# Weight loads and fp32 rows in pieces, each held until a step of the work (attention and squared-ReLU FFN on a normalised input)

## The chip, the core and the metric

The kernel runs on one core of a Trainium2 chip. Its engines are TensorE (PE, with its weight loads as PEld), VectorE (DVE), ScalarE (ACT), GpSimd (POOL) and SyncE (SP), which only issues transfers. The metric is the device time of one execution in microseconds (us). The median of three runs of the kernel before is 748.19 us (748.0 to 749.2).

## The reference

One layer norm feeds an attention with 32 query heads that share one key and one value head, and a feed-forward network with a squared ReLU; both are added to the input x. S = 2048 rows, D = 640, head size 20, F = 1536, all bfloat16.

```python
xn = layernorm(x)
q = (xn @ wq) in 32 heads of 20;  k = xn @ wk;  v = xn @ wv
p = softmax(q k^T / sqrt(20));    o = p v  -> [S, 640] @ wo
h = xn @ w1 + b1;  h = max(h, 0)**2;  ffn = h @ w2 + b2
out = x + attention + ffn
```

## The kernel before

The rows are cut in 16 tiles of 128 (st). For each, DVE or ACT takes mean and variance, POOL the inverse root, and DVE or POOL writes the normalised row tile XN. PE transposes it (T), and TE copies the transposed tile out of PSUM into xnT. From xnT come the keys (KT), the values (V) and the queries (QC), and by transfers on SP the queries of four heads at a time land in qT.

Attention works in 32 blocks of four heads and 512 query columns. A block has 16 key tiles; each gives four score tiles of 128 x 512. PE writes scores (`ps<-qT,kT`), ACT takes the exponential of two score tiles at once (128 x 1024, line 813, `PT<-ps`), PE multiplies with v (`ps<-PT,vx`). Some key tiles go another way: DVE reads the scores out of PSUM as a linear function into 16-bit integers (line 978), three shifted copies of these are made on DVE or POOL (line 996), and four matmuls with scaled values add up to the exponential. Which key tiles go there is decided while the order is made.

In between PE does the FFN: units FFN{qc}_{f} (w1, 12 for each of four groups of 512 rows; evacuated by RL on DVE, line 575, then squared by SQ), for the last group eight units FP (w2, evacuated by FE), which are kept in memory and added at the very end, and for the other groups OUT (w2 and wo together). FE and OUT add rows of x + b2 in fp32, which transfers XR (line 620) bring from an internal tensor `xbd`. A transfer on POOL's queue writes `xbd` with b2 in every row and converts to fp32 (XC, line 665); two more accumulate x on it (XB, line 666).

The order of all engines is worked out ahead by a planner in the program: it holds a list of open operations for each engine, gives each a planned duration, and commits the one that can start first, with priorities. The committed lists are what the chip executes, in that order on every engine, with semaphore waits between engines. So whatever alters one operation can shift the order of all that are committed after it. In the kernel before a load has no condition and is committed as soon as its engine's queue is free:

```python
l_w1 = load("w1", "SP", lambda e: e.dma_start(w1_sb[:], ...), 12.0)
x_32 = op("XC", "POOL", POOLDMA, lambda e: e.dma_start(xbd[:, :], ...), [xn_op[XCAT]], ...)
```

Of the kernel before, what the change touches and what calls it, by code (L numbers as in the profile page):

```python
# [164 lines left out]
def bass_parallel_sum__grouped_kv_mqa__dense_activation_squared_relu__prompt_kernel(nc, A_x, A_wq, A_wk, A_wv, A_wo, B_x, B_w1, B_b1, B_w2, B_b2, out):  # L165
    es = ExitStack()
    with es:  # L167
# [88 lines left out]
        def commit(op):  # L256
            s = start_of(op, op.ready())
            if op.eng == "PE":
                pe_mode[0] = op.mode
                pe_log.append((s, s + op.dur))  # L260
            op.start, op.fin = s, s + op.dur
            free[op.eng] = op.fin
            if op.lock:
                lock_free[0] = op.fin
            seq[op.eng].append(op)
            order_all.append(op)
            return op

        pe_log = []
# [8 lines left out]
            return b / WINDOW  # L278

        dve_q, pool_q, sp_q, act_q = [], [], [], []  # L280
        QUE = {"DVE": dve_q, "POOL": pool_q, "SP": sp_q, "ACT": act_q}
# [38 lines left out]
        l_wq = load("wq", "SP", lambda e: e.dma_start(wq_sb[:, :, 80:D], wqv[:, :, 80:D]), 10.0)  # L320
        l_w1 = load("w1", "SP", lambda e: e.dma_start(w1_sb[:], B_w1.rearrange("(p dt) f -> p dt f", p=128)), 12.0)
        l_b1 = load("b1", "SP", lambda e: e.dma_start(b1row[:], B_b1.rearrange("(f p) -> f p", p=128)), 12.0)
        l_w2 = load("w2", "SP", lambda e: e.dma_start(w2_sb[:], B_w2.rearrange("(ft p) d -> p ft d", p=128)), 14.0)
        woz = op("woz", "DVE", 0.4, lambda e: e.memset(wo7[:], 0.0), prio=-1)
        l_wo = [load("wo", "SP", lambda e: e.dma_start(wo_c[:], A_wo.rearrange("(c p) n -> p c n", p=128)), 14.0)]
        wos = one()
        l_wo7 = []
        for i in range(HPG):
            hh = H - HPG + i
            l_wo7.append(op("wo7", "SP", 0.5, lambda e, i=i, hh=hh: e.dma_start(wo7[32 * i:32 * i + DH, :], A_wo[DH * hh:DH * hh + DH, :]), [woz], lat=14.0, dma=wos))  # L330
# [108 lines left out]
        def need_te(sts):  # L439
            return [te_op[st] for st in sts]  # L440
# [126 lines left out]
        def unit_FFN1(qc, f):  # L567
            sts = range(4 * qc, 4 * qc + 4)
            ch = [(0.215, (lambda dt=dt: col4(lambda j: w1_sb[:, dt, f * 128 + 32 * j:f * 128 + 32 * j + 32], xnT[:, dt, qc * 512:(qc + 1) * 512], 512, dt, dt == DT - 1)))
                  for dt in range(DT)]  # L570

            def evac(p, bk):
                k = nffn[0]
                nffn[0] += 1
                o = Op(f"RL{qc}_{f}", "DVE", 0.66, [lambda e: e.tensor_scalar(out=hT_tmp[:, k % 2, :], in0=ps[:, bk, :], scalar1=b1col[:, f:f + 1], scalar2=0.0,  # L575
                                                                             op0=ALU.add, op1=ALU.max)], [p, b1_ev[0]] + ([ffn_sq[k - 2]] if k >= 2 else []))
# [12 lines left out]
            return Unit(f"FFN{qc}_{f}", ch, lambda: (qc == QC - 1 or all(8 * ((qc - 1) % QC) + i in fp_pe for i in range(8))) and has_te(range(ST)) and b1_ev[0] is not None,  # L589
                        evac, lambda: need_te(sts) + [l_w1])  # L590

        def out_mats(st, half, cks, with_ffn):
            qc, stl = st // 4, st % 4
# [22 lines left out]
        def xload(k):  # L616

            n = XORD[k]
            st, cs = n // 2, slice(n % 2 * HW, n % 2 * HW + HW)
            xr_op[n] = op(f"XR{n}", "SP", 0.45, lambda e: e.dma_start(xr[:, k % NXR, :], xbd[st * 128:(st + 1) * 128, cs]), [x_b2[st < 12], fp_ev.get(XORD[k - NXR]) if k >= NXR else None],  # L620
                          lat=2.2 + DMARG, dma=xrsem[k % NXR])

        def orow(st):
# [6 lines left out]
        def unit_FP(n):  # L630
# [5 lines left out]
            def evac(p, bk):  # L636
# [5 lines left out]
            return Unit(f"FP{n}", out_chunks(mats), lambda: all((qc, f) in sq_op for f in range(FT)) and n in xr_op, evac, lambda: [sq_op[(qc, f)] for f in range(FT)] + [l_w2])  # L642

        def unit_OUT(n):
            st, half = n // 2, n % 2
# [5 lines left out]
            def evac(p, bk):  # L651
# [10 lines left out]

        OT7 = QCr[:, 1, :]

        x_32 = op("XC", "POOL", POOLDMA, lambda e: e.dma_start(xbd[:, :], B_b2.rearrange("(o n) -> o n", o=1).to_broadcast([S, D])), [xn_op[XCAT]], lat=30.0, dma=one(), prio=3)
        x_b2 = [op(f"XB{k}", "POOL", POOLDMA, lambda e, r0=r0, r1=r1: e.dma_start(xbd[r0:r1, :], A_x[0][r0:r1, :], accum_op=ALU.add, max_dma_last_dim=4 * D), [x_32], lat=land, dma=one(), prio=3)
                for k, r0, r1, land in ((0, 1536, S, 22.0), (1, 0, 1536, 60.0))]
        for n in range(NXR):
            xload(n)

# [652 lines left out]
```

## Time and profile before

| what | value |
|---|---|
| median of three runs | 748.19 us |
| profiled execution, its own time | 747.4 us |
| its span, first to last instruction | 745.7 us |
| busy: PE, ACT, DVE, POOL | 97%, 94%, 86%, 56% of the span |
| exponentials on ACT (line 813) | 748, 689.0 us in sum |
| mean granted TensorE clock | 0.968 of full speed |
| moved by DMA | 44.23 MB, 59 GB/s on average |

PE's busy share is modelled from pipelined matmuls and says little of how close it is to its limit. In a list of groups the part after the bar is busy time and the mean of one in ns, then the idle time before them and what ended it. In a chain or a list of waits the columns are start (or total), duration, what. "issue" is time in which an engine waited for nothing that the profile shows. In a table by stretches each engine's busy time and count stands in the same order: PE, PEld, DVE, ACT, POOL, then the granted clock, the DMA share and GB/s. Queue 0 is POOL's, queue 1 SP's, queues 8 and 14 carry instructions. Names there are without numbers: `w_sb` is w1 or w2, `in_B_b_dram` b1 or b2.

### The profile page before, as it was taken

Reading aid. Unit: us, or ns where it says so; the run is one execution under the profiler, and the core shown is the slowest. Engines: PE = TensorE matmul, PEld = TensorE weight load, DVE = VectorE, ACT = ScalarE, POOL = GpSimd, SP = SyncE. Lnnn points to the kernel's source line nnn. Section 1 sums busy time; section 2 is a strip of 40 time slices with the busy share of each in tenths; the row PEclk is TensorE's granted clock in tenths of the full one; section 3 lists DMA queues with packets and bytes.
Section 4 is the critical chain, followed back from the end, with each engine's and each line's share of the span. In section 5 each row is a group of like instructions: output and inputs, shape, how many; then the busy total and the mean of one; then the engine's idle time right before and its main releaser. Section 6 shows DMA issues by size and latency. Waiting matters only on the chain.

```text
span 745.7 us, 22540 instructions
## 1 busy us (share of the span) xinstructions
PE 723.6 (97%) x9793; PEld 217.5 (29%) x9795; DVE 639.7 (86%) x1099; ACT 698.7 (94%) x770; POOL 418.2 (56%) x258
## 2 busy tenths in 40 slices
PE   7994999999999999999999999999999999999998
PEld 3230222333322223323322223332332222333323
DVE  5653798998989989899999999989999999959893
ACT  5673799999999999999999999999999999999994
POOL 4360356386567745667557665656556745546562
PEclk9586799999999999999999999999999999999999
DMA  9439594112211100111111011112110102121101
GB/s 319 135 92 145 79 224 121 35 54 71 55 38 28 28 19 19 51 37 37 45 47 26 15 28 29 37 29 54 46 47 21 33 20 85 37 55 38 30 20 46
DMA packets 39538, 44.23 MB, mean 59 GB/s; under 512 B 15412, under 2 KB 30004, under 8 KB 39184
## 3 DMA queue, kind: packets, MB, share of 16 engines
q1 hardware_dynamic: 34064, 31.84, 15.6%
q0 software_dynamic: 4144, 10.49, 7.2%
q8 instruction: 76, 1.25, 0.7%
q10 hardware_dynamic: 1232, 0.48, 0.2%
q14 instruction: 22, 0.18, 0.1%
HBM read 25.48 MB, written 14.93 MB: 54 GB/s over the span
## 4 chain that ended last, share of the span: by engine, by line
ACT 78%; PE 16%; DVE 2%; issue 2%; DMA 1%; ACTq 0%
ACT PT L813 78%; PE ps L294 15%; DMA wv_c<-in_A_wv_dram 1%; DVE tmore L978 1%; PE ps L467 1%; DVE x_sb L996 0%; DVE tmore L996 0%; DVE hT_tmp L575 0%; PE ps L495 0%; DVE xnT L470 0%; DVE big L583 0%; PE ps L402 0%; ACTq L167 0%; ACTq L309 0%; PE ps L423 0%
## 5 line engine op out<-in xcount | busy, mean ns | idle before, releaser
L813 ACT ACTIVATE PT<-ps 128x1024 bf16<-128x1024 f32 x748 | 689.0, 1172 | 31.1 <-PE ps L294 31.0
L978 DVE TENSOR_SCALAR tmore<-ps 128x512 uint16<-128x512 f32 x552 | 359.3, 684 | 46.0 <-PE ps L294 42.2
L294 PE MATMUL ps<-qT,kT 20*128 20x512 bf16 x2048 | 298.7, 391 | 3.0 <-ACT PT L813 1.8
L996 POOL TENSOR_SCALAR x_sb<-tmore 128x2048 uint16<-128x2048 uint16 x105 | 198.6, 1901 | 139.5 <-PE ps L294 38.2
L996 POOL TENSOR_SCALAR tmore<-tmore 128x2048 uint16<-128x2048 uint16 x102 | 192.7, 1897 | 145.8 <-DVE x_sb L996 50.9
L294 PEld LDWEIGHTS ps<-qT,kT 20*128 20x128 bf16 x2048 | 73.2, 91 | 301.5 <-ACT PT L813 288.1
L294 PE MATMUL ps<-PT,vx 128*32 128x512 bf16 x1496 | 142.6, 394 | 10.4 <-issue 9.5
L996 DVE TENSOR_SCALAR x_sb<-tmore 128x2048 uint16<-128x2048 uint16 x125 | 94.1, 778 | 0.0
L294 PE MATMUL ps<-x_sb,vxs 128*32 128x512 bf16 x920 | 82.2, 382 | 0.0
L294 PE MATMUL ps<-xnT,w_sb 128*32 128x512 bf16 x960 | 79.0, 394 | 0.1
L294 PE MATMUL ps<-w_sb,big 128*32 128x320 bf16 x1536 | 76.5, 302 | 0.0
L294 PE MATMUL ps<-tmore,vxs 128*32 128x512 bf16 x736 | 68.4, 386 | 0.0
L996 DVE TENSOR_SCALAR tmore<-tmore 128x2048 uint16<-128x2048 uint16 x82 | 59.6, 747 | 0.0
L294 PEld LDWEIGHTS ps<-PT,vx 128*32 128x32 bf16 x1496 | 35.9, 94 | 73.9 <-issue 69.8
L294 PE MATMUL ps<-tmore,vx 128*32 128x512 bf16 x552 | 54.4, 384 | 0.1
L294 PEld LDWEIGHTS ps<-w_sb,big 128*32 128x32 bf16 x1536 | 31.4, 95 | 31.0 <-issue 25.2
L575 DVE TENSOR_SCALAR hT_tmp<-ps,b1col 128x512 bf16<-128x512 f32 x48 | 35.7, 743 | 3.9 <-PE ps L294 3.6
L294 PE MATMUL ps<-xnT,wq_sb 128*32 128x512 bf16 (+1 forms) x480 | 36.9, 386 | 0.9 <-DMA wq_sb<-in_A_wq_dram 0.9
L294 PE MATMUL ps<-wo_c,OC 128*32 128x320 bf16 x640 | 31.7, 302 | 0.0
L539 DVE CAST QCr<-ps 128x512 bf16<-128x512 f32 x20 | 13.7, 687 | 15.9 <-PE ps L294 15.6
L294 PEld LDWEIGHTS ps<-x_sb,vxs 128*32 128x32 bf16 x920 | 21.6, 95 | 19.2 <-issue 13.8
L294 PEld LDWEIGHTS ps<-xnT,w_sb 128*32 128x32 bf16 x960 | 17.8, 95 | 28.3 <-issue 23.8
(79 smaller groups left out, 269.5 us busy)
## 6 DMA issues: line engine op xcount, KB each, us to landing
xbd<-in_B_b_dram POOLq DMA_DIRECT2D x1, 5120.0 KB, 39.1
xr<-xbd SPq DMA_DIRECT2D x32, 160.0 KB, 2.4
w_sb<-in_B_w_dram SPq DMA_DIRECT2D x2, 1920.0 KB, 15.5
xbd<-in_A_x_dram POOLq DMA_DIRECT2D x1, 3840.0 KB, 26.3
big<-OR SPq DMA_DIRECT2D x74, 40.0 KB
big<-drs SPq DMA_DIRECT2D x74, 40.0 KB
out_dram<-out_sb SPq DMA_DIRECT2D x15, 160.0 KB, 1.9
qT<-QCr SPq DMA_DIRECT2D x108, 20.0 KB
```

The source lines that it names most:

```text
L294: return lambda e: e.matmul(out_, l, r, start=start, stop=stop, tile_position=tp)
L467: return [(lambda e, dt=dt: e.transpose(out=psbf(bk)[:, dt * 128:(dt + 1) * 128], in_=xn_sb[:, st, dt:D:DT], identity=ident[:])) for dt in ...
L539: o = Op(f"QCe{qc}_{c}", "DVE", 0.60, [lambda e: e.tensor_copy(out=QCr[:, k % NQC, :], in_=ps[:, bk, :])], [p] + qc_dma.get(k - NQC, []))
L575: o = Op(f"RL{qc}_{f}", "DVE", 0.66, [lambda e: e.tensor_scalar(out=hT_tmp[:, k % 2, :], in0=ps[:, bk, :], scalar1=b1col[:, f:f + 1], scal ...
L813: return Op(f"ACT{st_['j']}", "ACT", 0.05 + 0.4267 * n, [lambda e: e.activation(out=PT[:, s0:s0 + n, :], in_=ps[:, b0:b0 + (n - 1) * db + ...
L978: d1 = op(f"D1_{n}_{i}", "DVE", 0.60, lambda e: e.tensor_scalar(out=L[:, cs].bitcast(U16), in0=ps[:, bank, :], scalar1=XA, scalar2=XB, op0 ...
L996: p = op(f"P{j}_{n}", eng, 0.60 if eng == "DVE" else 1.86, lambda e, T=T, j=j, two=two: e.tensor_scalar(out=T.bitcast(U16), in0=L.bitcast( ...
```

## The change

An operation may now name a step that must have been committed before it: it lies in `late` until then, and gets that step as a dependency, so that its engine also waits for it on the chip. The table HOLD names the steps. wq's rest waits for TE2, w1 (now four pieces) for TE4, TE6, TE8 and TE10, w2 (four) for RL3_2 to RL3_8, wo (two) for RL3_10 and FE24. The fp32 rows are made in another way: POOL converts b2 once into `b2d` (BC), 16 transfers on SP copy it to 128 rows of `xbd` each (XC), and 8 on POOL accumulate 256 rows of x each (XB); RL{qc}_{f} is the evacuation of an FFN unit, the group qc = 3 being the first.

```diff
-POOLDMA = 1.7
-XCAT = 7
+HOLD = dict(wq="TE2", b1="TE5", w1=("TE4", "TE6", "TE8", "TE10"), w2=("RL3_2", "RL3_4", "RL3_6", "RL3_8"), wo=("RL3_10", "FE24"), wo7="FE25", b2="VE8",
+            xc=[f"FE{24 + k}" for k in range(8)] + [f"RL0_{k}" for k in range(4)] + ["RL3_0", "RL3_1", "RL3_1", "RL3_2"],
+            xb=[f"RL0_{k}" for k in range(6)] + ["RL3_3", "RL3_5"])
@@ def op
-            QUE[eng].append(o)
+            ev = [d for d in o.deps if isinstance(d, str)]
+            if ev:
+                late.setdefault(ev[0], []).append(o)
+            else:
+                QUE[eng].append(o)
             return o
+        def released(ev):
+            for o in late.pop(ev.name, []):
+                o.deps[o.deps.index(ev.name)] = ev
+                QUE[o.eng].append(o)
@@ loads
-        l_wq = load("wq", "SP", ..., 10.0)
-        l_w1 = load("w1", "SP", lambda e: e.dma_start(w1_sb[:], B_w1.rearrange("(p dt) f -> p dt f", p=128)), 12.0)
+        l_wq = load("wq", "SP", ..., 8.0, [HOLD["wq"]])
+        l_w1 = [load(f"w1{k}", "SP", lambda e, k=k: e.dma_start(w1_sb[:, :, 384 * k:384 * k + 384], w1v[:, :, 384 * k:384 * k + 384]), 8.0, [HOLD["w1"][k]]) for k in range(4)]
-        l_w2 = load("w2", "SP", lambda e: e.dma_start(w2_sb[:], B_w2.rearrange("(ft p) d -> p ft d", p=128)), 14.0)
+        l_w2 = [load(f"w2{k}", "SP", lambda e, k=k: e.dma_start(w2_sb[:, 3 * k:3 * k + 3, :], w2v[:, 3 * k:3 * k + 3, :]), 8.0, [HOLD["w2"][k]]) for k in range(4)]
+        l_wo = [load(f"wo{c0}", ..., 8.0, [HOLD["wo"][k]]) for k, (c0, c1) in enumerate(((0, 3), (3, NCH)))]
@@ fp32 rows
-        x_32 = op("XC", "POOL", POOLDMA, lambda e: e.dma_start(xbd[:, :], B_b2...to_broadcast([S, D])), [xn_op[XCAT]], lat=30.0, ...)
-        x_b2 = [op(f"XB{k}", "POOL", POOLDMA, ..., accum_op=ALU.add, max_dma_last_dim=4 * D), [x_32], ...)
-                for k, r0, r1, land in ((0, 1536, S, 22.0), (1, 0, 1536, 60.0))]
+        b2_32 = op("BC", "POOL", 1.1, lambda e: e.dma_start(b2d[:], B_b2[:]), [HOLD["b2"]], lat=4.0, dma=one(), prio=3)
+        for st in range(ST):
+            x_b2[st] = op(f"XC{st}", "SP", 0.45, lambda e, st=st: e.dma_start(xbd[128 * st:128 * st + 128, :], b2d...to_broadcast([128, D])),
+                          [b2_32, HOLD["xc"][st]], lat=8.0, dma=one(), prio=3)
+        for st in range(0, ST, 2):
+            o = op(f"XB{st}", "POOL", 1.25, lambda e, r0=r0, r1=r1: e.dma_start(xbd[r0:r1, :], A_x[0][r0:r1, :], accum_op=ALU.add, ...),
+                   [x_b2[st], x_b2[st + 1], HOLD["xb"][st // 2]], lat=12.0, dma=one(), prio=3)
```

The order of SP's queue at the start of the program, before:

```order
L309 DMA x_sb<-in_A_x_dram 128x640 x2
L317 DMA x_sb<-in_A_x_dram 128x2x640 x2
L317 DMA x_sb<-in_A_x_dram 128x4x640 x2
L320 DMA wq_sb<-in_A_wq_dram 128x5x560
L321 DMA w1_sb<-in_B_w1_dram 128x7680
L322 DMA b1row<-in_B_b1_dram 12x128
L323 DMA w2_sb<-in_B_w2_dram 128x12x640
L325 DMA wo_c<-in_A_wo_dram 128x5x640
L330 DMA wo7<-in_A_wo_dram 20x640 x4
L556 DMA qT<-QCr 20x512 x2
```

The same place now, where wq and each piece of w1 waits for its step:

```order
L324 DMA x_sb<-in_A_x_dram 128x640 x2
L332 DMA x_sb<-in_A_x_dram 128x2x640 x2
L332 DMA x_sb<-in_A_x_dram 128x4x640 x2
L335 DMA wq_sb<-in_A_wq_dram 128x5x560
L337 DMA w1_sb<-in_B_w1_dram 128x5x384
L338 DMA b1row<-in_B_b1_dram 12x128
L337 DMA w1_sb<-in_B_w1_dram 128x5x384 x2
L574 DMA qT<-QCr 20x512 x2
```

w2 and wo have left the start, and w1 stands there in pieces. Further on in SP's queue, at the second group of queries, before:

```order
L556 DMA qT<-QCr 20x512 x6
L556 DMA qT<-QCr 4x512
L556 DMA qT<-QCr 16x512
L556 DMA qT<-QCr 20x512 x5
L556 DMA qT<-QCr 12x512
L882 DMA drs<-OR 4x512
L893 DMA big<-OR 20x512 x4
L883 DMA R4<-drs 128x16
```

The same place now; `xbd<-b2d` is one of the 16 copies, `drs`, `big` and `R4` belong to the normalisation of a block:

```order
L574 DMA qT<-QCr 20x512 x6
L574 DMA qT<-QCr 4x512
L686 DMA xbd<-b2d 128x640
L574 DMA qT<-QCr 16x512
L574 DMA qT<-QCr 20x512 x5
L574 DMA qT<-QCr 12x512
L686 DMA xbd<-b2d 128x640 x2
L907 DMA drs<-OR 4x512
L918 DMA big<-OR 20x512 x4
L340 DMA w2_sb<-in_B_w2_dram 128x3x640
L686 DMA xbd<-b2d 128x640
L908 DMA R4<-drs 128x16
```

Four copies and the first piece of w2 now stand among the transfers of queries and of the first block's normalisation. On POOL, behind the scaled values (`vxs`), before:

```order
L453 TENSOR_SCALAR vxs<-vx 128x128 x2
L665 DMA xbd<-in_B_b2_dram 2048x640
L453 TENSOR_SCALAR vxs<-vx 128x128 x9
L996 TENSOR_SCALAR x_sb<-tmore 128x2048
L996 TENSOR_SCALAR tmore<-tmore 128x2048 x2
L666 DMA xbd<-in_A_x_dram 512x640
L666 DMA xbd<-in_A_x_dram 1536x640
```

and now:

```order
L471 TENSOR_SCALAR vxs<-vx 128x128 x2
L683 DMA b2d<-in_B_b2_dram 16x40
L471 TENSOR_SCALAR vxs<-vx 128x128 x9
L1021 TENSOR_SCALAR tmore<-tmore 128x2048 x2
L1021 TENSOR_SCALAR x_sb<-tmore 128x2048
L1021 TENSOR_SCALAR tmore<-tmore 128x2048
L690 DMA xbd<-in_A_x_dram 256x640
L1021 TENSOR_SCALAR tmore<-tmore 128x2048
L1021 TENSOR_SCALAR x_sb<-tmore 128x2048 x2
L690 DMA xbd<-in_A_x_dram 256x640
```

In place of the broadcast over 2048 rows stands one row, and the accumulations come in pieces of 256 rows between the shifted copies. The planner's order of the first 99 groups on PE is the same as before; later it differs, and ACT has 744 exponentials of 128 x 1024 where it had 748 (DVE 560 reads of scores where it had 552).

More of the change, by code (lines that the diff above doesn't have):

```diff
@@ L224, in bass_parallel_sum__grouped_kv_mqa__dense_activation_squared_relu__prompt_kernel @@
         xbd = nc.dram_tensor("xbd", [S, D], F32, kind="Internal").ap()
+        b2d = nc.dram_tensor("b2d", [D], F32, kind="Internal").ap()
         fpd = nc.dram_tensor("fpd", [128, 8, HW], F32, kind="Internal").ap()
@@ L266, in commit @@
             order_all.append(op)
+            released(op)
             return op
@@ L280, in bass_parallel_sum__grouped_kv_mqa__dense_activation_squared_relu__prompt_kernel @@
         dve_q, pool_q, sp_q, act_q = [], [], [], []
+        late = {}
         QUE = {"DVE": dve_q, "POOL": pool_q, "SP": sp_q, "ACT": act_q}
@@ L589, in unit_FFN1 @@
             return Unit(f"FFN{qc}_{f}", ch, lambda: (qc == QC - 1 or all(8 * ((qc - 1) % QC) + i in fp_pe for i in range(8))) and has_te(range(ST)) and b1_ev[0] is not None,
-                        evac, lambda: need_te(sts) + [l_w1])
+                        evac, lambda: need_te(sts) + [l_w1[f // 3]])
         def out_mats(st, half, cks, with_ffn):
@@ L619, in xload @@
             st, cs = n // 2, slice(n % 2 * HW, n % 2 * HW + HW)
-            xr_op[n] = op(f"XR{n}", "SP", 0.45, lambda e: e.dma_start(xr[:, k % NXR, :], xbd[st * 128:(st + 1) * 128, cs]), [x_b2[st < 12], fp_ev.get(XORD[k - NXR]) if k >= NXR else None],
+            xr_op[n] = op(f"XR{n}", "SP", 0.45, lambda e: e.dma_start(xr[:, k % NXR, :], xbd[st * 128:(st + 1) * 128, cs]), [x_b2[st], fp_ev.get(XORD[k - NXR]) if k >= NXR else None],
                           lat=2.2 + DMARG, dma=xrsem[k % NXR])
@@ L641, in evac @@
                 return o
-            return Unit(f"FP{n}", out_chunks(mats), lambda: all((qc, f) in sq_op for f in range(FT)) and n in xr_op, evac, lambda: [sq_op[(qc, f)] for f in range(FT)] + [l_w2])
+            return Unit(f"FP{n}", out_chunks(mats), lambda: all((qc, f) in sq_op for f in range(FT)) and n in xr_op, evac, lambda: [sq_op[(qc, f)] for f in range(FT)] + l_w2)
         def unit_OUT(n):
@@ L663, in bass_parallel_sum__grouped_kv_mqa__dense_activation_squared_relu__prompt_kernel @@
         OT7 = QCr[:, 1, :]
-        x_32 = op("XC", "POOL", POOLDMA, lambda e: e.dma_start(xbd[:, :], B_b2.rearrange("(o n) -> o n", o=1).to_broadcast([S, D])), [xn_op[XCAT]], lat=30.0, dma=one(), prio=3)
-        x_b2 = [op(f"XB{k}", "POOL", POOLDMA, lambda e, r0=r0, r1=r1: e.dma_start(xbd[r0:r1, :], A_x[0][r0:r1, :], accum_op=ALU.add, max_dma_last_dim=4 * D), [x_32], lat=land, dma=one(), prio=3)
-                for k, r0, r1, land in ((0, 1536, S, 22.0), (1, 0, 1536, 60.0))]
+        b2_32 = op("BC", "POOL", 1.1, lambda e: e.dma_start(b2d[:], B_b2[:]), [HOLD["b2"]], lat=4.0, dma=one(), prio=3)
+        x_b2 = {}
+        for st in range(ST):
+            x_b2[st] = op(f"XC{st}", "SP", 0.45, lambda e, st=st: e.dma_start(xbd[128 * st:128 * st + 128, :], b2d.rearrange("(o n) -> o n", o=1).to_broadcast([128, D])),
+                          [b2_32, HOLD["xc"][st]], lat=8.0, dma=one(), prio=3)
+        for st in range(0, ST, 2):
+            r0, r1 = 128 * st, 128 * st + 256
+            o = op(f"XB{st}", "POOL", 1.25, lambda e, r0=r0, r1=r1: e.dma_start(xbd[r0:r1, :], A_x[0][r0:r1, :], accum_op=ALU.add, max_dma_last_dim=4 * D),
+                   [x_b2[st], x_b2[st + 1], HOLD["xb"][st // 2]], lat=12.0, dma=one(), prio=3)
+            x_b2[st] = x_b2[st + 1] = o
         for n in range(NXR):
```

11 lines of the change are left out of this document (7 added, 4 removed).

## The prediction

> **What bounds the kernel now.** I read the page first, then the chain in order of time, then the waits of ScalarE (ACT), then clock and busy time by stretches, then the DMA queues around the two places where the chain says "issue".
>
> ```profile
> span 745.7 us, 22540 instructions
> PE 723.6 (97%) x9793; PEld 217.5 (29%) x9795; DVE 639.7 (86%) x1099; ACT 698.7 (94%) x770; POOL 418.2 (56%) x258
> q8 instruction: 76, 1.25, 0.7%
> L813 ACT ACTIVATE PT<-ps 128x1024 bf16<-128x1024 f32 x748 | 689.0, 1172 | 31.1 <-PE ps L294 31.0
> L575 DVE TENSOR_SCALAR hT_tmp<-ps,b1col 128x512 bf16<-128x512 f32 x48 | 35.7, 743 | 3.9 <-PE ps L294 3.6
> ...
> 2.88 7.63 DMA wv_c<-in_A_wv_dram
> ...
> 16.32 1.97 issue
> ...
> 57.29 9.50 issue
> ...
> 102.57 529.11 ACT PT L813 x577
> ```
>
> The 748 exponentials on ACT carry the time: in the chain 577 of them stand back to back in 529.11 us, 0.917 us each. The rest of ACT's time is waiting, nearly all for TensorE (PE). The next rows are that wait, first of the whole span, then of 19 to 45.4, 47 to 120 and 110 to 746 us; below them the first and the last group of ACT and the one that follows the long hole.
>
> ```profile
> ACT PT L813 <- PE ps L294: 31.0, 29, 9.7
> ...
> ACT PT L813 <- PE ps L294: 13.3, 14, 3.1
> ...
> ACT PT L813 <- PE ps L294: 16.4, 13, 9.7
> ...
> ACT PT L813 <- PE ps L294: 1.3, 2, 1.1
> ...
> 18.94 2.85 ACT L813 ACTIVATE PT<-ps 128x1024 bf16<-128x1024 f32 x3 [3.10 <-PE ps L294]
> 67.98 1.02 ACT L813 ACTIVATE PT<-ps 128x1024 bf16<-128x1024 f32 x1 [9.67 <-PE ps L294]
> 682.62 53.27 ACT L813 ACTIVATE PT<-ps 128x1024 bf16<-128x1024 f32 x58 [1.10 <-PE ps L294]
> ```
>
> So the span splits into: 18.9 before the first exponential; 748 x 0.917 = 685.9 of work; 27.9 of waits after the start (31.0 less the 3.1 that lie before 18.94): 10.2 before 45.4, 16.4 around the hole, 1.3 late; 3.2 because an exponential that stands alone shows 1.02 us where the dense ones advance by 0.917; and 9.8 from the last one's end (735.9) to 745.7. The run with this profile took 747.4 us, 1.7 above its span; the median of the runs, 748.19, is another 0.8 above.
>
> Why PE is late shows in the stretches: time, PE, PEld, DVE, ACT, POOL busy, granted clock, DMA share, GB/s.
>
> ```profile
> 0.00:2.00 2.00, 0.48 (x2) 0.21 (x3) 0.33 (x1) 0.00 (x0) 1.35 (x11) 1.00 0.09 10
> 16.00:18.00 2.00, 0.32 (x13) 0.14 (x12) 0.49 (x1) 0.00 (x0) 0.71 (x1) 1.00 0.91 353
> 18.00:20.00 2.00, 1.30 (x22) 0.85 (x23) 1.37 (x5) 1.06 (x2) 0.55 (x1) 0.94 1.05 359
> 20.00:42.00 22.00, 21.98 (x160) 6.04 (x164) 12.17 (x45) 14.74 (x15) 9.13 (x14) 0.50 0.28 93
> 45.00:57.00 12.00, 11.57 (x153) 4.20 (x153) 8.35 (x16) 11.62 (x13) 4.60 (x9) 1.00 0.51 147
> 62.00:84.00 22.00, 17.21 (x126) 3.09 (x128) 8.71 (x14) 10.25 (x11) 1.90 (x1) 0.50 1.11 147
> 86.00:102.00 16.00, 15.62 (x197) 4.12 (x193) 15.82 (x27) 16.00 (x18) 7.90 (x5) 1.00 0.46 103
> 110.00:630.00 520.00, 518.91 (x7066) 150.09 (x7058) 480.36 (x785) 520.00 (x568) 319.92 (x171) 1.00 0.16 41
> ```
>
> Twice PE has a hole (1.97 and 9.50 us) and right behind it the granted clock is 0.50 for over 20 us; there PE is the bound and ACT waits about half a microsecond before each exponential. At clock 1.00 (45:57, 86:102, 110:630) ACT hardly waits. And at both holes PE waits for no semaphore ("issue"). What is in the DMA queues then: first 13 to 17 us, then 43 to 57, then 57 to 67, then the landing of one issue.
>
> ```profile
> q1 hardware_dynamic: 149, 1.68, 100.3%
> q8 instruction: 1, 0.02, 1.6%
> ...
> q0 software_dynamic: 680, 1.74, 42.7%
> q1 hardware_dynamic: 122, 0.08, 2.8%
> ...
> q0 software_dynamic: 568, 1.45, 95.4%
> q8 instruction: 1, 0.02, 0.6%
> ...
> xbd<-in_B_b_dram POOLq DMA_DIRECT2D x1, 5120.0 KB, 39.1
> ```
>
> Queue 8 brings instructions: 1.25 MB over PE's 9793 + 9795 instructions is 64 B each, so one of its 76 packets (16.4 KB) feeds about 128 matmuls with their loads. I infer it is PE's. In 45:57 PE used 153 matmuls, more than a packet, yet from 43 to 57 none arrived; one came in 57 to 67, and PE resumed. All that while the 5120 KB broadcast of b2 (39.1 us to land) filled queue 0. At 16 us the packet stood among w1, w2 and wo. So the holes read as late instruction packets behind bulk transfers. In 110:630 the DMA share is 0.16 and PE has no such hole.
>
> The Trainium skill, "Runtime: NRT & Kernel Launch", section "Instruction fetch mechanics", says that an engine's sequencer drives its own DMA queue for 16 KiB blocks and that crossing a block is mostly hidden. The packet size agrees; "hidden" does not hold in 57 to 67 us if my reading is right, and by that sentence alone the hole would have another cause and stay, which is the fourth rival.
>
> **The change, part by part.**
>
> ```profile
> xbd<-in_A_x_dram POOLq DMA_DIRECT2D x1, 1280.0 KB, 8.9
> wq_sb<-in_A_wq_dram SPq DMA_DIRECT2D x1, 700.0 KB, 10.2
> fpd<-OC SPq DMA_DIRECT2D x8, 160.0 KB, 1.9
> w_sb<-fpd SPq DMA_DIRECT2D x1, 1280.0 KB, 6.0
> L666 POOL DMA_DIRECT2D xbd<-in_A_x_dram x2: 1549/2262/2976, 93.0 to 93.9; - x2
> L665 POOL DMA_DIRECT2D xbd<-in_B_b_dram x1: 1279/1279/1279, 43.6 to 43.6; - x1
> ```
>
> *Weights held.* Ahead of the first exponential the queue now carries x, wk, wv and the first columns of wq; the rest of wq waits for TE2, w1 for TE4 to TE10, w2, wo for later. The packet needed at 16.3 us then meets at most wq (700 KB) and a first 480 KB of w1, against 1.68 MB that moved in 13 to 17 us alone. I take the whole 1.97 off (ends: 0 and 1.97), nearer the upper one because in 20:42, where the queues drain (share 0.28), PE is busy 21.98 of 22 us. wv_c lands 7.63 us after its issue beside wq and w1; that is at 10.5 us. Without them sooner: x, wk, wq's first columns and wv are 2.8 MB by their shapes, at the 1.68 MB in 4 us shown above 6.6 us, from 2 us on (nothing moves before), so 8.6; between 0 and 1.9 us. I take 0.5, as wq's first columns stand before wv and x's 2.6 MB beside both. First exponential: 18.9 - 2.0 - 0.5 = 16.5 (15.0 to 18.9).
>
> *The early half clock* goes with the hole, since it starts in the stretch behind it and nothing else idles PE there. PE's 22 us at 0.50 are then some 11 to 12 us against 14.7 of ACT. ACT's early waits fall from 10.2 to 2.5; ends 0.4 (the 0.38 in 45:57) and 5.1 (half), because DVE and POOL, with 12.17 and 9.13 us of work in 22, get close to full when the stretch shrinks to 15.
>
> *The broadcast* of 5120 KB becomes b2 once as fp32 (2.5 KB) and 16 copies of 320 KB on SP, plus 8 accumulations of 640 KB on POOL, each at its own step. The FFN steps that release them are far apart: 48 FFN units and 32 output units share the span, 745.7 / 80 = 9 us on average. A 320 KB copy takes by the 160 and 1280 KB rows about 1.9 to 6.0 us, an accumulation by the 1280 KB row about half of 8.9. Three copies stand close together (RL3_0 and RL3_1), 960 KB, under 6.0 us. PE uses a packet in 520 / 7066 x 128 = 9.4 us, so a delay under that is covered if a packet is asked for one ahead. Hence the 9.50 hole and the half clock behind it go: waits 16.4 to 1.0 (0 as in 86:102, up to 2).
>
> *POOL and SP.* POOL issues 9 DMAs instead of 3: 8 x 1.5 to 3.0 us against 5.8 before, so 7 to 18 us more on an engine with 327 us idle. SP gets 23 more issues, each able to hold back the qT and normalisation transfers behind it. I cost both at 0 on the path: cover is POOL's idle time and slack of later blocks; without it, the 7 to 18 us.
> *Late weights* cost 0. The next rows are TE4, which releases w1's first piece, the first matmul of the later blocks' queries, which reads the held part of wq, and the first that reads w1:
>
> ```profile
> 14.57 0.47 DVE L470 COPY xnT<-ps 128x640 bf16<-128x640 bf16 x1
> ...
> 29.62 1.04 PE L294 MATMUL ps<-xnT,wq_sb 128*32 128x512 bf16 x8
> ...
> 54.50 0.39 PE L294 MATMUL ps<-xnT,w_sb 128*32 128x512 bf16 x4
> ```
>
> For w1 40 us lie between, some 30 when the early spell is gone, for 480 KB; the next pieces are asked for in steps of two TEs, and FFN units come 9 us apart on average. wq is tightest: after TE2, which follows wv's 10.5 us, it has until about 23 us with the early spell gone, against 10.2 us at its worst in the crowd.
>
> *The new order* has 744 exponentials instead of 748 (four more pieces of 1024 go to VectorE, 8 more of its 0.684 us reads): 4 x 0.917 = 3.7 less for ACT. DVE has 480 of 520 us in the dense stretch and takes 7 us more over the span: 0.
>
> Sum for the span: 16.5 + 744 x 0.917 (682.2) + waits 2.5 + 1.0 + 1.3 (late ones kept) + 1.0 for lone exponentials + 9.8 = 714.3. With 1.7 and 0.8: 716.8, say **717 us**, 31 below 748.2 (4.2%).
>
> **Rivals.**
> 1. *The early half clock stays*, because PE still idles enough there (a packet a little late, rows of the layer norm late). For it: the drop came after only 1.97 us idle; DVE and POOL work close by. Against: nothing idles PE in 14 to 16 us. Then 16.5 + 682.2 + 10.2 + 1.0 + 1.3 + 2.1 + 9.8 + 2.5 = 725.6. The Trainium skill, "TensorE: Matmul & The Clock Gate", Part 1, wants an idle window of about 3.4 us for half rate and about 3.4 us of work to leave it. The trace differs on both (0.32 + 1.30 busy of 4 us, then 22 us at 0.50 with PE 21.98 busy); by that page a 2 us hole would not be the cause and removing it would leave the drop, which is this case's time.
> 2. *The spread traffic still holds a packet* around the first FFN units, where three copies, w2's pieces and an accumulation meet. A hole of 2 us brings the half clock and its 6.7 us of waits (16.4 less 9.67), so 717 - 1 + 8.7 = 724.7; the whole old hole again 732.4. Middle 728.
> 3. *Slower.* One held copy at the head of SP's queue keeps the qT loads behind it (the copy for rows 12 stands ahead of seven of them), and PE has no queries. It decides when these loads come later than their block by more than 32 us in sum; 16 copies would each have to cost ACT 2 us. Against: late transfers cost ACT nothing visible in 110:630. At least 750.
> 4. *The holes are not fetches*: only the four exponentials are won, 748.2 - 3.7 = 744.5. Against: the queue rows above.
>
> **How the numbers follow.** Forecast 0.68 (own range 712 to 723), rival 1 0.13, rival 2 0.11, rival 4 0.04, rival 3 0.03, no change 0.01. The low end takes 15.0 for the start, waits 0.4 + 0 + 1.0 and 0.5: 711. The high end takes in rival 1 and half of rival 2: 730. All but rival 3 and the last are faster by more than 0.2%, which is about what a measurement of this kernel tells from no change: faster 0.95, same 0.02, slower 0.03.
>
> **What would show it.** In the profile after: no "issue" of microseconds in the chain before 100 us; granted clock 1.00 from 16 to 100; first exponential near 16.5; ACT's wait for PE near 8 in all (3 before the start, 5 after); 744 exponentials at 0.917; queue 8 packets at even distances in 40 to 70 us. A clock of 0.50 in 20:42 alone is rival 1, one around 45 to 75 rival 2, waits of ACT for PE with SP's queue behind a held copy rival 3, a 9 us hole at the same matmul rival 4.

## The result, and the profile after

The changed kernel takes 718.28 us (median of four executions, 717.74 to 719.99), the kernel before 748.1 (746.91 to 749.2) beside it: a ratio of 0.961 (95% interval 0.958 to 0.963), 29.8 us less. The forecast was 717 (711 to 730). The profiled execution took 717.74 us. A median and a range below are of all executions of a kernel; where single ones lie more than 1.5% above the least, the ratio leaves these out.

First the page of the kernel after: its span, the engines, queue 8 and the group of exponentials (now line 838).

```profile
span 716.0 us, 22581 instructions
PE 703.5 (98%) x9781; PEld 215.2 (30%) x9783; DVE 643.5 (90%) x1109; ACT 692.4 (97%) x766; POOL 428.8 (60%) x268
q8 instruction: 76, 1.25, 0.7%
L838 ACT ACTIVATE PT<-ps 128x1024 bf16<-128x1024 f32 x744 | 682.7, 1174 | 3.5 <-PE ps L309 3.5
```

ACT waits for PE 3.5 us in the whole span, where it waited 31.0. The chain that ended last (start, duration, what) has no "issue" of microseconds any more; nearly all of it is ACT, the exponentials still 0.917 us apart (395.20 / 431).

```profile
2.88 7.11 DMA wv_c<-in_A_wv_dram
...
16.28 1.01 ACT PT L838
...
33.18 46.84 ACT PT L838 x51
...
121.51 395.20 ACT PT L838 x431
...
704.00 0.40 issue
704.41 1.25 DVE OC L931 x2
...
705.71 7.52 PE ps L309 x166
```

The stretches of the holes and of the half clock before (PE, PEld, DVE, ACT, POOL busy, granted clock, DMA share, GB/s):

```profile
16.00:18.00 2.00, 1.57 (x24) 0.84 (x21) 2.00 (x8) 1.74 (x2) 0.72 (x2) 1.00 0.88 247
20.00:42.00 22.00, 21.57 (x287) 8.70 (x283) 15.90 (x52) 20.02 (x23) 15.98 (x26) 1.00 0.24 63
45.00:57.00 12.00, 11.80 (x153) 3.11 (x145) 10.49 (x19) 12.00 (x15) 3.36 (x2) 1.00 0.21 61
62.00:84.00 22.00, 21.81 (x273) 5.76 (x270) 20.53 (x37) 22.00 (x25) 11.61 (x8) 1.00 0.70 182
```

The clock is 1.00 in all four, and in 20:42 PE does 287 matmuls where it did 160. The DMA share in 62:84 is still 0.70, but in pieces. Queue 8's packets (the start of each transfer in the trace) come at 12.6, 17.7, 25.6, 34.5, 44.6, 55.5 and 69.2 us; before, they came at 15.7, 23.0, 30.7, 64.5 and 82.1, with nothing between 30.7 and 64.5. The waits of ACT and the end of its work, then VectorE and PE behind it, in order of time (start, duration, group, idle time before it):

```profile
16.26 14.96 ACT L838 ACTIVATE PT<-ps 128x1024 bf16<-128x1024 f32 x16 [0.95 <-PE ps L309]
33.16 57.85 ACT L838 ACTIVATE PT<-ps 128x1024 bf16<-128x1024 f32 x63 [1.94 <-PE ps L309]
670.23 31.27 ACT L838 ACTIVATE PT<-ps 128x1024 bf16<-128x1024 f32 x34 [0.18 <-PE ps L309]
...
703.77 0.71 DVE L903 STREAM_TRANSPOSE QCr<-QCr 128x512 bf16<-128x512 bf16 x1
704.41 1.24 DVE L931 TENSOR_TENSOR OC<-big 128x512 bf16<-128x512 f32 x2
...
705.11 1.05 PE L309 MATMUL ps<-wo_c,OC 128*32 128x320 bf16 x8 [2.75 <-DVE OC L931]
```

The last exponential ends at 701.50 and the span at 716.0: 14.5 us of tail, where it was 9.8. PE stands 2.75 us for the two multiplies that make the last columns of OC, and right behind that (705.0 to 708.5) its clock is 0.50. It is the one place found where the new kernel is slower than the old.

### The profile page after: what moved, and what is told of

It reads as the page before. It is cut to its first block, busy times and chain, and to the rows that moved or that the text cites. A ratio compares the mean times of both kernels' runs of the same rounds, so it can differ in the third digit from the quotient of the medians.

```text
span 716.0 us, 22581 instructions
## 1 busy us (share of the span) xinstructions
PE 703.5 (98%) x9781; PEld 215.2 (30%) x9783; DVE 643.5 (90%) x1109; ACT 692.4 (97%) x766; POOL 428.8 (60%) x268
## 4 chain that ended last, share of the span: by engine, by line
ACT 81%; PE 17%; DMA 1%; DVE 1%; ACTq 0%; issue 0%; DVEq 0%
ACT PT L838 81%; PE ps L309 16%; DMA wv_c<-in_A_wv_dram 1%; PE ps L485 0%; DVE OC L931 0%; PE ps L513 0%; PE ps L420 0%; ACTq L169 0%; ACTq L324 0%; DVE OR L897 0%; PE ps L441 0%; DVE QCr L899 0%; PE ps L455 0%; ACTq L329 0%; DVE PT L1237 0%
## 5 line engine op out<-in xcount | busy, mean ns | idle before, releaser
L838 ACT ACTIVATE PT<-ps 128x1024 bf16<-128x1024 f32 x744 | 682.7, 1174 | 3.5 <-PE ps L309 3.5
L1021 POOL TENSOR_SCALAR tmore<-tmore 128x2048 uint16<-128x2048 uint16 x110 | 207.7, 1898 | 152.3 <-DVE x_sb L1021 41.0
L309 PE MATMUL ps<-qT,kT 20*128 20x512 bf16 x2048 | 290.7, 384 | 2.3 <-ACT PT L838 1.7
L1021 POOL TENSOR_SCALAR x_sb<-tmore 128x2048 uint16<-128x2048 uint16 x101 | 190.4, 1897 | 99.9 <-PE ps L309 31.6
L309 PE MATMUL ps<-PT,vx 128*32 128x512 bf16 x1488 | 137.3, 386 | 0.5 <-DVE OR L905 0.4
L309 PE MATMUL ps<-xnT,w_sb 128*32 128x512 bf16 x960 | 77.3, 384 | 0.0
L309 PE MATMUL ps<-wo_c,OC 128*32 128x320 bf16 x640 | 34.0, 311 | 2.9 <-DVE OC L931 2.8
L309 PE MATMUL ps<-xnT,wq_sb 128*32 128x512 bf16 (+1 forms) x480 | 33.2, 356 | 0.7 <-DMA wq_sb<-in_A_wq_dram 0.7
L601 DVE TENSOR_TENSOR big<-hT_tmp 128x512 bf16<-128x512 bf16 x48 | 24.4, 523 | 0.0
```

The lines of the kernel that those rows point to most:

```text
L309: return lambda e: e.matmul(out_, l, r, start=start, stop=stop, tile_position=tp)
L838: return Op(f"ACT{st_['j']}", "ACT", 0.05 + 0.4267 * n, [lambda e: e.activation(out=PT[:, s0:s0 + n, :], in_=ps[:, b0:b0 + (n - 1) * db + ...
L1021: p = op(f"P{j}_{n}", eng, 0.60 if eng == "DVE" else 1.86, lambda e, T=T, j=j, two=two: e.tensor_scalar(out=T.bitcast(U16), in0=L.bitcast( ...
```

## Experiments

All are read against the kernel before on the same chip. Unless said otherwise an edit is to the kernel after.

### 1 and 2: each half of the change alone

`e1_weights_held` keeps the weights held in pieces and makes the fp32 rows as before; `e2_rows_pieces` makes the rows in pieces and loads the weights whole and at once.

```diff
 e1
-        b2_32 = op("BC", ...);  16 x XC on SP;  8 x XB on POOL
+        x_32 = op("XC", "POOL", ..., lambda e: e.dma_start(xbd[:, :], B_b2...to_broadcast([S, D])), [xn_op[XCAT]], ...)
+        x_b2 = [op(f"XB{k}", "POOL", ...) for k, r0, r1, land in ((0, 1536, S, 22.0), (1, 0, 1536, 60.0))]
 e2
-        l_w1 = [load(f"w1{k}", ..., [HOLD["w1"][k]]) for k in range(4)]   # and wq, w2, wo, wo7
+        l_w1 = load("w1", "SP", lambda e: e.dma_start(w1_sb[:], ...), 12.0)
```

> One part alone: the weights in held pieces, the fp32 rows as before (one broadcast of 5120 KB on POOL, two accumulations); 748 exponentials. Theory (an instruction packet of PE waits behind bulk transfers, and the hole brings the half clock): the 1.97 us hole at 16 us is gone, first exponential at 16.3, clock 1.00 from 16 to 40 us; the broadcast, now issued near 32 us, still holds a packet back, a hole of 5 to 12 us somewhere between 40 and 65 us with 'issue' before it, then 20 to 24 us at 0.50. 735 us (730 to 742). Rival (the gain is from the new order and has nothing to do with packets): no hole follows the broadcast, 718 to 722.

> The other part alone: the fp32 rows in held pieces, the weights whole and at the start as before; 744 exponentials. Theory: the hole of about 2 us at 16 us and the half clock from 20 to 43 us are back, first exponential at 18.9 and some 10 us of waits before 45 us; no hole after that. 731.5 us (728 to 735). Rival (order): 718 to 722 with the clock at 1.00 from 20 to 42; rival (the early half clock has its own cause): as the theory.

Weights alone: 739.98 (733.32 to 743.58), ratio 0.989 (0.984 to 0.995). Rows alone: 731.55 (722.55 to 732.56), ratio 0.976 (0.970 to 0.982). From both kernels, the chain's hole and the first exponential behind it (start, duration, idle before); e1 first, then e2:

```profile
55.02 5.24 issue
...
61.87 1.02 ACT L832 ACTIVATE PT<-ps 128x1024 bf16<-128x1024 f32 x1 [6.01 <-PE ps L310]
```

```profile
16.56 2.14 issue
...
19.36 2.85 ACT L835 ACTIVATE PT<-ps 128x1024 bf16<-128x1024 f32 x3 [3.27 <-PE ps L309]
```

Each half removes its own hole and leaves the other's. So the early hole belongs to the weights and the late one to the rows. The late hole is only 5.24 us in e1, yet the clock stays at 0.50 for 44.4 us behind it, longer than the 23.9 us before and the 20 to 24 expected. In stretches of 3.41 us, from the hole to the end of the spell:

```profile
53.33:56.73 3.40, 1.69 (x21) 0.34 (x18) 2.38 (x5) 2.53 (x3) 1.90 (x1) 1.00 1.13 190
56.74:60.15 3.41, 0.00 (x0) 0.00 (x0) 0.00 (x0) 0.00 (x0) 0.00 (x0) 0.50 1.15 183
60.16:63.56 3.40, 3.31 (x25) 0.62 (x28) 0.83 (x2) 1.19 (x2) 1.90 (x1) 0.50 1.54 170
...
97.70:101.11 3.41, 3.41 (x30) 0.66 (x27) 1.49 (x3) 2.05 (x2) 2.30 (x2) 0.50 0.58 171
101.12:104.52 3.40, 3.40 (x48) 0.87 (x44) 3.00 (x5) 3.15 (x4) 3.31 (x2) 1.00 0.00 0
```

The clock drops at the end of a stretch in which PE was busy 1.69 of 3.40 us, and stays down through the next thirteen stretches, in twelve of which PE is busy nearly all the time. One execution of e2 took 722.55 with a mean clock of 0.993, where the other three have 0.977 to 0.979. Only the times and mean clocks of these executions are known; 9 us is what escaping the early spell would explain, by rival 1's own 8.6.

### 3 to 5: the hold or the split?

`e5_split_not_held` keeps the pieces of the weights and lets all of them go behind one step. `e6_held_not_split` loads w1, w2 and wo whole, each held until the step of its first piece. `e9_w1_split_only` is e2 with w1 alone in its four pieces of columns (rows of 768 B instead of 15360 B), unheld.

```diff
 e5
-HOLD = dict(wq="TE2", b1="TE5", w1=("TE4", "TE6", "TE8", "TE10"), w2=("RL3_2", ...), wo=("RL3_10", "FE24"), wo7="FE25", b2="VE8",
+HOLD = dict(wq="X12", b1="X12", w1=("X12",) * 4, w2=("X12",) * 4, wo=("X12", "X12"), wo7="X12", b2="VE8",
 e6
-        l_w1 = [load(f"w1{k}", ..., w1v[:, :, 384 * k:384 * k + 384]), 8.0, [HOLD["w1"][k]]) for k in range(4)]
+        l_w1 = [load("w1", "SP", lambda e: e.dma_start(w1_sb[:], w1v), 8.0, [HOLD["w1"][0]])] * 4
 e9, against e2
-        l_w1 = load("w1", "SP", lambda e: e.dma_start(w1_sb[:], ...), 12.0)
+        l_w1 = [load(f"w1{k}", "SP", ..., w1v[:, :, 384 * k:384 * k + 384]), 12.0) for k in range(4)]
```

> The changed kernel, fp32 rows as changed, weights in the same pieces, but all released at the start (behind the last load of x). Theory (it is the holding that counts: the packet at 16 us waits behind all that is queued): hole of about 2 us at 16 us and half clock from 20 to 44 us, as in the run with the rows alone: 731.5 us, or 722 where the clock's window does not see the hole. Rival (the splitting counts, as short runs let the instruction packet pass): hole under 1 us, clock 1.00, 718 to 721.

> The changed kernel with w1, w2 and wo each in one transfer (1920, 1920, 800 KB), held until the step of their first piece. Theory (a packet is asked for about 9 us ahead, so a transfer that lands in about 6 us holds nothing up): 718.3 us within 2. Rival (whole weights in long rows hold a packet back): a hole of 1 us or more and half clock, 726 or more.

> The run with the rows alone (e2: weights at the start, hole of 2 us at 16 us, 731.6 us) with one thing altered: w1 in four column pieces (rows of 768 bytes) instead of one transfer (rows of 15360 bytes), still unheld at the same place of the queue; wq, w2, wo whole. Theory (formed after the split weights without holding came to 718.9: long rows of w1 keep an engine of the DMA busy so that the instruction packet arrives late): packet before 13.5 us, no hole, clock 1.00, 718.5 us (717 to 720). Rival (it is the amount queued): as e2, 731.5.

e5: 718.91 (718.28 to 719.88), ratio 0.961 (0.958 to 0.964), as the changed kernel and not the 731.5 expected. But the experiment does not say what it was made for. X12 is the load of the last four row tiles of x, and SP waits for its landing before it issues the weights:

```profile
11.50 0.70 SPq L335 DMA_DIRECT2D wq_sb<-in_A_wq_dram  x1
12.24 4.43 SPq L337 DMA_DIRECT2D w_sb<-in_B_w_dram  x4
```

So it was a hold too, to 11.5 us. What it does show: full DMA queues alone are not enough for a hole. From 16 to 30 us the DMA share is 1.02 to 1.11, as full as in e2's 16 to 20 us (0.99), but queue 8's packets come at 12.8, 19.7 and 28.0 and PE has no hole.

e9 is the unheld split, for w1: the four pieces are issued from 4.58 us on, and the hole is there:

```profile
4.58 8.75 SPq L337 DMA_DIRECT2D w_sb<-in_B_w_dram  x4
...
15.72 2.57 issue
```

731.58 (730.44 to 736.54), ratio 0.981 (0.974 to 0.988), against e2's 731.55. The expected 718.5 was missed: the first packet comes at 15.9 us, as in the kernel before (15.7), where the changed kernel has 12.6. The length of the rows is not what delays the packet here, and splitting w1 without holding it gains nothing. (The profiled execution is that of 736.54, and its clock is 0.95 where it is not halved; the mean clocks of the other three, 0.977 to 0.981, are near those of e2.)

e6 gave 719.37, 726.38, 737.77 and 740.94, at mean clocks of 0.995, 0.988, 0.968 and 0.965 (median 732.08, against 747.63 for the kernel before). The profiled one is that of 719.37; it has no hole, and its second packet comes at 20.9 us where the changed kernel has 17.7. The expected 718.3 was missed: held whole loads are sometimes as good and mostly not. The lower clocks say that more half clock came in the longer ones; where, no trace shows. In the traces, then, the hold is what removes the early hole (e5 and e6 have none, e9 has one); that the pieces are what makes it certain fits e5's even times against e6's, and is not shown beyond that.

### 6 to 9: how much bulk, and on which queue

`e3_bulk_5120` and `e12_bulk_1280` add to the kernel after, behind BC on POOL's queue, a converting broadcast that nobody reads, of 5120 and 1280 KB. `e11_bulk_act` adds 5120 KB as a plain fp32 copy on ACT's queue. `e7_rows_at_once` releases the 16 copies together and the 8 accumulations together.

```diff
 e3 (e12: [0:512] and 512)
+        dumd = nc.dram_tensor("dumd", [S, D], F32, kind="Internal").ap()
+        dum = Op("DUM", "POOL", 0.0, [lambda e: e.dma_start(dumd[0:2048, :], B_b2...to_broadcast([2048, D]))], dma=one())
+        order_all.insert(order_all.index(b2_32) + 1, dum)
 e11
+        dum = Op("DUM", "ACT", 0.0, [lambda e: e.dma_start(dumd[:, :], b2d...to_broadcast([S, D]))], [b2_32], dma=one())
+        order_all.insert([o.name for o in order_all].index("XC12") + 1, dum)
 e7
-            xc=[f"FE{24 + k}" for k in range(8)] + ..., xb=[f"RL0_{k}" for k in range(6)] + ["RL3_3", "RL3_5"])
+            xc=["RL3_0"] * 16, xb=["RL3_3"] * 8)
```

> The changed kernel in its own order, plus one transfer that nobody reads: b2 broadcast to 2048 fp32 rows (5120 KB) into a scratch tensor, on POOL behind the conversion of b2, waited for only at the very end. Theory: it lands after about 39 us, an instruction packet that is asked for meanwhile comes late, a hole of 5 to 12 us before 75 us with 'issue', 0.50 of clock behind it: 734 us (727 to 746). Rival (holes depend on the order or on who waits for the rows): no hole, 718.3 within 2 us.

> The changed kernel with the unread converting broadcast on POOL cut to 512 rows (1280 KB instead of 5120). Theory (a packet is asked for about 9 us ahead): it lands in about 10 us, so a packet comes at most just in time: 718.3 to 721, no hole over 0.5 us. Rival (any such broadcast makes a hole): 726 or more with half clock.

> The changed kernel with an unread copy of b2 to 2048 fp32 rows (5120 KB), as the bulk run, but plain (already fp32) and on ACT's own queue, issued once behind the exponentials of about 50 us. Theory (any bulk holds the instruction packet): hole of 3 to 12 us with 'issue', half clock, 735 us (728 to 750). Rival (a packet of another queue gets its turn; only the converting transfer of POOL's queue holds it): no hole of 'issue', 719 to 722; small transfers of SP may be late.

> The changed kernel with all 16 copies of b2 released at RL3_0 and all 8 accumulations at RL3_3; 748 exponentials (3.7 us more by that). Theory: 5120 KB and then as much again stand in the queues, the copies alone 16 us or more by 960 KB in some 4 us, so an instruction packet comes more than 9 us late: hole of 2 to 10 us between 50 and 110 us, half clock behind it, 737 us (728 to 750). Rival (plain copies of SP's queue, without conversion, let an instruction packet pass): no hole, 722 us.

e3: 750.0 (743.5 to 757.07), ratio 1.001 (0.994 to 1.008): the unread broadcast alone gives back the whole gain. Its hole, the first wait, and ACT's wait in all, then queue 8 in the kernel after (43 to 57 us) and all that the queues of e3 carried from 45 to 57 us:

```profile
56.29 3.58 issue
...
62.04 1.02 ACT L838 ACTIVATE PT<-ps 128x1024 bf16<-128x1024 f32 x1 [4.54 <-PE ps L309]
...
ACT PT L838 <- PE ps L309: 25.8, 36, 4.5
...
q8 instruction: 2, 0.03, 1.0%
...
q0 software_dynamic: 645, 1.65, 68.4%
q1 hardware_dynamic: 584, 0.44, 48.5%
```

Queue 8's packets come at 34.9 and then at 57.2 us, none in the 45 to 57 us shown; in the kernel after, two fall in that time (44.6 and 55.5). The mechanism came as expected and the size did not: 734 (727 to 746) was expected, and the half clock lasted 54.6 us (58.5 to 113.1).

e12: 719.55 (718.49 to 719.97), ratio 0.963 (0.956 to 0.971). The packet comes at 47.8 instead of 44.6, 3 us late, and PE does not notice. So a packet may be some microseconds late, but not the twelve of e3: one is asked for ahead, as the prediction assumed. The trace of the kernel after shows how far: its packet of 44.6 us starts when PE has done 597 matmuls and 599 loads, and in e3 PE stops without it after 731 and 732, about one packet's content (128) later.

e11: 763.21 (759.32 to 778.34), ratio 1.020 (1.012 to 1.028), and e7: 772.17 (770.2 to 789.28), ratio 1.031 (1.026 to 1.036). e11 has no "issue" hole on PE and e7 a single one of 0.91 us, at 77 us; for e11 neither expected time came. Instead two transfers of 8 KB in the first block's normalisation stand in the chain (in the kernel after, the transfers that read or write `drs` take 1.4 to 4.5 us); e11's chain, then its first exponential behind them, then the same of e7:

```profile
65.53 16.97 DMA drs<-OR
...
82.52 21.26 DMA R<-drs
...
105.95 1.02 ACT L838 ACTIVATE PT<-ps 128x1024 bf16<-128x1024 f32 x1 [30.64 <-PE ps L309]
```

```profile
81.81 20.02 DMA drs<-OR
...
101.85 14.60 DMA R<-drs
...
119.48 1.02 ACT L837 ACTIVATE PT<-ps 128x1024 bf16<-128x1024 f32 x1 [39.08 <-PE ps L308]
```

For e7 an instruction hole of 2 to 10 us and 737 were expected; that theory failed. What came is close to the prediction's rival 3: transfers of data are late, and PE has nothing to multiply for 38.04 us, until 117.33. The clock is 0.50 from 79.5 to 154.6, so for 37 us more after PE is back. In e7 bulk and small transfers share SP's queue; in e11 the bulk is on another queue and the small ones take 17 and 21 us all the same. So the pieces need their distances, not only their size: e7 moves the same pieces as the changed kernel, at once, and is 54 us slower than it (3.7 of these for its four more exponentials).

The plain copies hold queue 8 back as well. Its fifth and sixth packets are 18.4 us apart in e7 and 19.2 in e11, against 11.0 in the kernel after, so 7 to 8 us late; e3's 22.3 us between the fourth and fifth, against 10.1, are 12 us late. The 9.4 us that PE takes for a packet lie between the two. So the conversion is not shown to be what makes the hole: in e11, and but for 0.91 us in e7, PE ran out of data before it ran out of instructions.

### 10: dense work against the half clock

`e10_burst` is e1 with 40 matmuls of zeros on PE (10 fills) put into its order behind QK47's next PV, where I expected the half clock to have begun.

```diff
+        at = next(o for k, o in enumerate(pes) if k > k0 and o.name[:2] == "PV")   # k0: QK47
+        for _ in range(10):
+            order_all.insert(order_all.index(at) + 1, Op("fill", "PE", 0.215, fill_parts()))
```

> The run with the weights alone held (e1: hole of 5 us near 56 us, half clock for 44 us, 740 us) plus ten groups of four matmuls of zero weights (40 matmuls, they add nothing to the sum in their bank) on PE some six exponentials behind the hole, 4.3 us at half clock. Theory (the half clock ends behind a stretch of 3.4 us that is denser than the 22 to 26 matmuls that PE and ACT manage together): the clock is 1.00 within 7 us of the burst, near 75 us instead of 101; 17 exponentials win 0.6 us each, less the burst: 733 us (729 to 736). Rival (the half clock lasts its time whatever PE does): 742 to 744.

734.58 (731.18 to 736.18), ratio 0.983 (0.976 to 0.990), against e1's 739.98 (733.32 to 743.58): the number came, but the trace does not carry the reason. In the profiled execution:

```profile
61.88:65.28 3.40, 3.40 (x30) 0.49 (x22) 2.52 (x4) 2.41 (x3) 0.95 (x1) 0.50 1.61 166
65.29:68.69 3.40, 3.40 (x52) 0.91 (x48) 2.73 (x5) 3.30 (x4) 0.00 (x0) 1.00 1.46 145
...
69.95 1.89 PE L310 MATMUL ps<-kT,zeros 128*32 128x512 bf16 x30
...
75.04 1.07 PE L310 MATMUL ps<-kT,zeros 128*32 128x512 bf16 x10 [3.20 <-issue]
```

The clock is back at 65.3 us, 4.7 us before the first zero is multiplied. So the burst did not end that spell, and the test of dense work is inconclusive. Why it ended after two steps of 3.41 us, where e1 with the same order up to the burst took thirteen, no trace shows; with it the cause of the gain over e1 stays open. (e1's steps hold 25 to 30 matmuls, so the theory's 22 to 26 was too low.) The trace shows something else. With the clock back and 40 more matmuls to fetch, PE came to the end of its packet at 71.84, before the next was there (queue 8 at 57.7 and 72.6, 15 us apart under the broadcast), and stood a second time, 3.20 us; a second spell of 0.50 follows (75.5 to 89.2). In e1 PE ran slowly enough that the packet of 71.9 came in time. It agrees with the fetch as the cause of the holes: PE used its instructions faster here and met a hole that e1 did not have.

### 11 and 12: the tail

`e4_tail_first` moves the two multiplies of OC (CM) ahead of the last block's transposes on DVE. `e8_tail_both` does that and also gives PE its order of before: 80 matmuls with wo_c, then those with wo7.

```diff
 e4 and e8
+        cms = [o for o in order_all[order_all.index(tn_op[NBLK - 1]):] if o.name[:2] == "CM"]
+        # each is put ahead of tn_op[NBLK - 1]
 e8
-            while ended <= k and (k == 7 or tb_op[(qc, NCH)].fin + LATS[("DVE", "PE")] <= free["PE"] + 0.02):
+            while ended <= k and (k == 7 or k >= 3 and tb_op[(qc, NCH)].fin + LATS[("DVE", "PE")] <= free["PE"] + 0.02):
```

> The changed kernel with the last two multiplications of the normalisation (OC<-big, line 931) moved on DVE from behind the last block's transposes to ahead of them. Theory (the tail of 14.5 us, against 9.8 before, comes from that order: PE stands 2.75 us for them and then runs at half clock): 3 us less, 715.2 us (714 to 717). Rival (their data lands only when they run now, so the last block's transposes are late instead): 718.3 within 1 us, or above.

> The changed kernel with the two last multiplications ahead of the last block's transposes on DVE, and on PE the first four output groups' wo matmuls (80) ahead of the first that needs the last block (16), as the kernel before had it. Theory (in the run with the first alone PE still stood 1.91 us for the last block and the clock halved): no hole over 1 us and no half clock in the tail, which is 10 us as before: 713.9 us (713 to 715.5). Rival (the tail's length is set by the last block's chain on DVE alone): 717 within 1 us.

e4: 717.28 (715.53 to 717.82), ratio 0.959 (0.956 to 0.962); about 1 us of the expected 3. The wait moved to the transposed block, and the half clock stayed in three of four executions by their mean clocks (0.997, 0.998, 0.998, 1.000 for 715.53):

```profile
704.93 0.46 PE L309 MATMUL ps<-wo,QCr 128*32 128x320 bf16 x4 [1.91 <-DVE QCr L903]
```

e8: **713.16** (712.11 to 714.3, six executions), ratio 0.953 (0.951 to 0.956), as expected (713.9), and 5.1 us under the changed kernel; the ranges do not touch. Its span, its last exponentials, the two multiplies, now ahead, and PE without a wait behind them:

```profile
span 711.4 us, 22582 instructions
...
670.27 31.27 ACT L838 ACTIVATE PT<-ps 128x1024 bf16<-128x1024 f32 x34 [0.18 <-PE ps L309]
...
698.75 0.69 DVE L931 TENSOR_TENSOR OC<-big 128x512 bf16<-128x512 f32 x1 [3.56 <-DMA big<-drs]
701.20 0.68 DVE L931 TENSOR_TENSOR OC<-big 48x512 bf16<-48x512 f32 x1 [1.75 <-DMA big<-drs]
...
701.91 2.89 PE L309 MATMUL ps<-wo_c,OC 128*32 128x320 bf16 x80
704.67 0.73 PE L309 MATMUL ps<-wo,QCr 128*32 128x320 bf16 x16
```

From 701.54 to 711.4 are 9.9 us of tail. This is the best version that ran.

## Why the prediction was right, and where it was not

The sum of 714.3 for the span, term by term, against the 716.0 measured in the profiled execution:

| term | forecast | after |
|---|---|---|
| first exponential | 16.5 | 16.26 |
| exponentials | 682.2 | 682.7 busy |
| waits after the start | 2.5 + 1.0 + 1.3 | 2.5 |
| lone exponentials | 1.0 | in the 682.7 |
| tail | 9.8 | 14.5 |

- *The holes are late instruction packets.* Right. The unread broadcast of e3 brings a hole back into a kernel that has none, and nothing reads that broadcast, and only SP waits for it, at the very end. This also decides against rival 4. Two readings of the traces say that these packets are PE's. In all nine "issue" holes (two in the kernel before and in e10, one in e1, e2, e3, e7 and e9) PE resumes 1.3 to 1.6 us after the end of a packet of queue 8. And PE stops at the same place of its program whatever the time: after 731 matmuls and 732 loads in e1, e3 and e10, after 223 and 223 in e2 and e9, and in e10 a second time 127 and 127 further on, a packet's content. The Trainium skill, "Runtime: NRT & Kernel Launch", section "Instruction fetch mechanics", calls the crossing of a block mostly hidden: it is in the kernel after, with 76 packets and no such hole, and is not in e1 (5.24 us) and e3 (3.58 us).
- *Weights held.* Right, start and all: wv_c lands 7.11 us after its issue instead of 7.63, the 0.5 that was taken. The text spoke of the amount that stands in the queue. In e5 the whole weights were queued from 11.5 us on, behind x, and no hole came; its first packet (12.8 us) was as early as in the changed kernel. So what counted was that this packet did not meet them.
- *The early half clock* went with its hole; rival 1 did not come. Its rule, that a 2 us hole is not the cause, is answered by e2: hole back (2.14 us), half clock back (20.3 to 44.2).
- *The broadcast.* Right, with the waits at its place not 1.0 but nearly nothing: of the 2.5 us left, 1.94 is the one wait at 33.16, where the early 2.5 was given, and the late 1.3 is down to 0.2 at 670. The term "late ones kept" was wrong by that: I took a wait of the old order for one of the new. With the clock at 1.00 in 45:57 and 62:84, rival 2 did not come.
- *Rival 3* was given 0.03 with "late transfers cost ACT nothing visible in 110:630" against it. For the released steps as they are that held. e7 shows that late transfers can cost more than the whole change gains, when the pieces go together: SP takes 22.0 us there to issue the 16 copies, and the loads of qT and the normalisation's transfers stand behind them.
- *POOL and SP* cost nothing visible on the path. The size given for POOL was too high: its nine transfers take 9.0 us to issue, 0.8 to 1.3 us each, against 5.8 for three before, so 3.2 more where 7 to 18 was given. (POOL's busy time is up by 10.6 us, mostly for its shifted copies of 1.9 us each, 211 in place of 207.)
- *The step that failed* is "+ 9.8 (the tail)". The sum took the tail over unchanged, though the order of the planner differs late in the program, as the section on the change says. After it, DVE makes the last columns of OC behind the last transposes, and PE reaches the wo7 matmuls early; PE waits 2.75 us and draws a half clock, 14.5 in place of 9.8. e8, which puts both back, has 9.9. The error of +4.7 there was in part covered by the waits that were 2.3 too many and by smaller terms, so that the sum came within 1.7 us of the span is in part luck.

What stays open: why e6's longer executions fell to the half clock; how a transfer on one queue holds up a packet or a small transfer on another, and whether the conversion has a part in it; and what ends a spell of half clock.

## What to carry to other kernels

Where an engine shows "issue" in the chain, look at the instruction queue's packets over that time: bulk transfers are then better cut in pieces and given out over the work, at distances that let a packet and the small transfers of data through (here 1280 KB at once did no harm, 5120 KB cost the whole gain). A hole of 2 to 5 us on TensorE is not priced by its length but by the half clock behind it: with it, e2, e1 and e3 are 13, 22 and 32 us over the changed kernel. And when a planner makes the order, the tail is to be read anew after every edit: it changes there too, where nothing covers it.

## What the runs showed of the hardware

The half clock mostly lasts longer than the hole that starts it, with PE busy nearly all the time once it has resumed: 23.9 us (e2), 44.4 (e1), 54.6 (e3), 75.1 (e7, of which PE stands for 37.8), 6.8 and 13.7 (e10), each a whole number of steps of 3.41 us (7, 13, 16, 22, 2, 4). It begins after a step in which PE was busy about half or less (1.69 of 3.40 us in e1, 0 to 1.7 in the other runs); the one exception is e7, where it was 2.30. The Trainium skill, "TensorE: Matmul & The Clock Gate", Part 1, has about 3.4 us as the window, which agrees, and about 3.4 us of work as enough to return, which does not: twelve such steps with PE busy passed in e1. In e1 PE did 25 to 30 matmuls in each of these steps, and no count of them parts the last from the others.

Transfers of 8 KB were 17 and 21 us on their way while 5120 KB moved on another engine's queue (e11); in the kernel after, the transfers of that tile take 1.4 to 4.5 us.
